# A delta-rule layer with a gated convolution: chunks of 32 tokens with the batches on four partition quadrants, in place of chunks of 64 with pairs of heads on two halves

## The chip, the core and the metric

The kernel runs on one core of a Trainium2 chip. The metric is the device time of one execution in microseconds (us). A core has five engines that run side by side, each through its own instructions in a fixed order: TensorE (PE, matrix products; its weight loads are listed as PEld), VectorE (DVE), ScalarE (ACT), GpSimd (POOL) and SyncE (SP, which here only issues DMA transfers). PE writes to PSUM, which this kernel uses in tiles of 128x512 (called banks in the code); ACT and DVE move results from there to SBUF. An fp32 product of the program appears in the trace as two matmul records, each with a weight load of its own; "record" below means one of these.

## The reference

Four batches, eight heads, 768 tokens, head size 48. A state matrix for each batch and head is read by the query and then corrected with the key and value of the token; what the queries read is the input of a gate, a causal convolution of five taps over tokens, applied to a projection.

```python
for t in range(S):
    kt, vt, bt = (k_n[:, :, t], v[:, :, t], beta[:, :, t, None])
    y[:, :, t] = np.einsum('bhd,bhde->bhe', q[:, :, t], state)
    v_old = np.einsum('bhde,bhd->bhe', state, kt)
    state = state + bt[:, :, :, None] * np.einsum('bhd,bhe->bhde', kt, vt - v_old)
...
for k in range(K):
    gate_pre += conv_w[k][None, None, :] * xp[:, k:k + S, :]
gate = 1.0 / (1.0 + np.exp(-gate_pre))
val = x @ w_val
return (gate * val @ w_out).astype(np.float32)
```

Here k_n is k divided by its length, and x is y with the eight heads side by side, 384 features a token.

## The kernel before

The loop over tokens is replaced by a loop over chunks. Inside a chunk the corrections of all tokens solve a triangular system, whose matrix comes from products of keys with keys (the gram). With the inverse of that matrix in hand a chunk needs four products: e, what the state says of the keys, taken off the values; u, the inverse applied to that; S, the state's update with keys and u; y, the queries on the state plus the masked products of queries and keys on u.

**Tiling.** A chunk is 64 tokens, and there are 12. Two heads share the 128 partitions, one on each half, so that 16 pairs (NP) stand along the free dimension. Two chunks make a group (128 tokens), and there are six groups.

**prep(g)** makes the inverses of a group. gram (L452, and gram0 for the first group) multiplies keys by keys and queries, and gevac copies the result to GL. diag picks the 32x32 diagonal blocks, trans_in turns them so that each partition of TLP holds one block per row of 1024 elements. Then the inverse TT_ is built on the free dimension: coef and cscale scale by beta over the squared length, row (L493) inverts blocks of 8, mergez8 and merget8 join them to 16, and zmul, zred, tmul and tred (L525 to L548) join 16 to 32, by a product with up to 1024 elements a partition and a sum over it. Some of the large products stand on POOL (buffers D1 and PR2), the others on DVE. trans_out turns the result twice, to TTR and TNA, and lev1 and lev2 join the 32-blocks to 64 on PE. bdcopy and tevac write the inverse to BD.

**chain(ch)** is the recurrence of one chunk: emul, eevac, umul, uevac, smul, sevac for the state, ymul and yevac for the output. Each product stands for one pair and one half; on PE two of them lie in different halves of the array. y comes out with features on partitions. yevac writes three quarters of it to X, and six DMA transfers a chunk (kind Lx) bring the rest to its partitions.

**moe(ch)** is the gate and the projection of a chunk: conv is tap 0 on ACT, tap is taps 1 to 3 on DVE (L783), tap_product on ACT and tap_sum on POOL (L790) are tap 4, sig the sigmoid, val (L798) nine products of 256 columns, gate (L802) the multiplication on DVE, outp (L809) six products of 384 columns, oevac the copy to SBUF, and then the output DMAs.

plan_weights turns the weights, which come as 64-bit numbers, into fp32: five steps on DVE and ACT, then f64_join, two multiplications and additions on POOL (L381, L382) for each of seven pieces.

**What sets the order.** Plan records every operation with its engine, an estimated cost and its tokens (what it reads and writes). Plan.order goes through the operations in time with these costs and puts on each engine, of those that are ready, the one with the highest rank (the longest way to the end plus a number of the table BIAS). The result is one fixed order for each engine. Where PE would stand idle, or has done little for some time, the planner adds keep_warm (L853), a product of zeros that changes nothing.

## Time and profile before

| what | value |
|---|---|
| median of 3 runs | 411.38 us (410.1 to 411.98) |
| span of the profiled execution | 416.2 us, 1.2% above that median |
| mean granted TensorE clock in it | 0.881 |
| PE, DVE, ACT, POOL busy | 352.4, 324.6, 233.7, 172.4 us |
| keep_warm among PE's time | 416 records, 62.6 us |
| moved by DMA | 45.31 MB, mean 109 GB/s; 44,576 of 59,805 packets under 512 bytes |

How to read it: PE's 352.4 us hold the fillers and whatever ran at a lowered clock, so they are not all work. A group's row in the profile gives the time in which at least one of its instructions ran, then the mean of one instruction; for products that lie in different parts of the array the first is far below the sum of the second.

### The profile page before, as it was taken

To read this page: it belongs to the slowest core of one execution; us is meant where nothing else is said; L and a number is where in the kernel's file an instruction comes from. 1 tells how busy PE (TensorE), PEld (TensorE's weight loads), DVE (VectorE), ACT (ScalarE), POOL (GpSimd) and SP (SyncE) were. 2 spreads that over 40 slices of the span, in tenths; PEclk is the share of its full clock that TensorE was granted. 3 is DMA by queue.
4 is the path that set the end of the run, shared out by engine and by line. 5 is a ranking of instruction groups with operands and counts; after the bars stand their busy time and mean duration, and the time that the engine had idled before them with its cause. 6 is when DMAs were issued, how large, how long until landed. Compare 5 with 4: busy or idle time off the path is not lost.

```text
span 416.2 us, 13720 instructions
## 1 busy us (share of the span) xinstructions
PE 352.4 (85%) x5836; PEld 297.6 (71%) x5836; DVE 324.6 (78%) x576; ACT 233.7 (56%) x509; POOL 172.4 (41%) x138
## 2 busy tenths in 40 slices
PE   8849967997499969989798999597599793999995
PEld 6849967886398738767586877476578593878883
DVE  5689999998894998988988379989587999320550
ACT  8403327966386636957377765353777364876420
POOL 4263650837802727505663233557023477100200
PEclk9985695999557969989989599989699997999999
DMA  7996561559273507354745545625303451010211
GB/s 222 166 251 198 157 183 50 145 151 192 52 151 116 142 14 157 104 122 139 154 106 157 128 130 142 106 61 131 49 2 79 78 114 24 2 41 13 48 39 38
DMA packets 59805, 45.31 MB, mean 109 GB/s; under 512 B 44576, under 2 KB 47776, under 8 KB 59744
## 3 DMA queue, kind: packets, MB, share of 16 engines
q1 hardware_dynamic: 59744, 44.43, 45.5%
q8 instruction: 46, 0.75, 0.8%
q14 instruction: 15, 0.12, 0.1%
HBM read 38.52 MB, written 4.72 MB: 104 GB/s over the span
## 4 chain that ended last, share of the span: by engine, by line
PE 52%; DVE 21%; DMA 11%; issue 6%; ACT 4%; SPq 3%; POOL 2%; DVEq 0%; POOLq 0%; ACTq 0%
PE gram L455 9%; PE SPS L853 9%; PE val L798 9%; PE out L809 8%; DVE GT L783 6%; PE u L713 4%; SPq L304 3%; DVE TTR L552 2%; DMA GL<-in_kq_dram 2%; PE SPS L725 2%; DMA AQ<-in_conv_w_dram 2%; PE z L564 2%; DVE TT__85 L547 2%; PE gram L465 2%; DVE PR L508 2%
## 5 line engine op out<-in xcount | busy, mean ns | idle before, releaser
L783 DVE SCALAR_TENSOR_TENSOR GT<-X,CW,GT 128x256 f32<-128x256 f32 x111 | 73.1, 684 | 12.9 <-POOL GT L790 12.2
L790 POOL TENSOR_TENSOR GT<-GT,TP 128x256 f32<-128x256 f32 x33 | 27.0, 817 | 97.7 <-ACT TP L299 97.4
L853 PE MATMUL SPS<-ZW 128*128 128x128 f32 x416 | 62.6, 309 | 0.0
L853 PEld LDWEIGHTS SPS<-ZW 128*128 128x128 f32 x416 | 58.5, 220 | 2.7 <-issue 1.0
L798 PE MATMUL val<-X,WV 128*128 128x256 f32 x216 | 58.9, 415 | 1.0 <-ACT BD L299 1.0
L809 PE MATMUL out<-WO,GT 128*128 128x384 f32 x144 | 52.1, 511 | 6.8 <-DVE GT L802 6.7
L455 PE MATMUL gram<-KQ,KBD 96*128 96x128 f32 x320 | 54.5, 331 | 0.8 <-DMA KQ<-in_kq_dram 0.8
L455 PEld LDWEIGHTS gram<-KQ,KBD 96*128 96x128 f32 x320 | 49.0, 237 | 2.3 <-ACT BD L299 0.9
L798 PEld LDWEIGHTS val<-X,WV 128*128 128x128 f32 x216 | 41.2, 203 | 7.6 <-ACT BD L299 1.1
L802 DVE TENSOR_TENSOR GT<-val,GT 128x256 f32<-128x256 f32 x36 | 15.0, 420 | 39.4 <-PE val L798 32.7
L575 ACT ACTIVATE BD<-TTR 32x512 f32<-32x512 f32 x48 | 30.1, 628 | 27.2 <-DVE TTR L552 26.7
L809 PEld LDWEIGHTS out<-WO,GT 128*128 128x128 f32 x144 | 27.4, 198 | 24.6 <-DVE GT L802 7.7
L449 POOL TENSOR_TENSOR US<-VT,NRM 64x768 f32<-64x768 f32 x24 | 36.4, 1516 | 19.7 <-DMA VT<-in_vt_dram 10.7
L299 ACT ACTIVATE GL<-gram 128x512 f32<-128x512 f32 x48 | 27.9, 594 | 23.4 <-PE gram L455 15.9
L793 ACT ACTIVATE GT<-GT 128x256 f32<-128x256 f32 x36 | 14.7, 415 | 43.4 <-DVE GT L783 43.1
L564 PE MATMUL z<-TTR,GL 32*32 32x32 f32 x768 | 12.0, 210 | 29.8 <-DVE TTR L552 21.6
L682 POOL TENSOR_SCALAR_AFFINE_SELECT AQ<-GL 64x1024 f32<-64x1024 f32 x24 | 28.7, 1195 | 15.4 <-PE y L739 8.9
L564 PEld LDWEIGHTS z<-TTR,GL 32*32 32x32 f32 x768 | 9.6, 123 | 34.0 <-DVE TTR L552 15.5
L713 PEld LDWEIGHTS u<-VT,BD 128*64 128x64 f32 x704 | 26.4, 157 | 9.5 <-ACT BD L299 4.5
L713 PE MATMUL u<-VT,BD 128*64 128x48 f32 x704 | 29.0, 242 | 4.5 <-ACT BD L299 3.6
L739 PE MATMUL y<-AQ,US 112*64 112x64 f32 x384 | 28.2, 226 | 1.8 <-ACT X L299 1.8
L299 ACT ACTIVATE OS<-out 128x384 f32<-128x384 f32 x24 | 11.8, 490 | 30.4 <-PE out L809 26.7
(116 smaller groups left out, 794.3 us busy)
## 6 DMA issues: line engine op xcount, KB each, us to landing
KBD<-in_kbd_dram SPq DMA_DIRECT2D x40, 192.0 KB, 3.1
KQ<-in_kq_dram SPq DMA_DIRECT2D x40, 192.0 KB, 3.3
KT<-in_kt_dram SPq DMA_DIRECT2D x12, 384.0 KB, 4.7
AQ<-in_qf_dram SPq DMA_DIRECT2D x24, 192.0 KB, 4.4
VT<-in_vt_dram SPq DMA_DIRECT2D x12, 384.0 KB, 3.7
out_dram<-OS SPq DMA_DIRECT2D x48, 96.0 KB, 2.2
KF<-in_kf_dram SPq DMA_DIRECT2D x22, 192.0 KB, 4.7
GL<-in_kq_dram SPq DMA_DIRECT2D x4, 448.0 KB, 9.6
```

Of the source, the lines that this page charges most:

```text
L299: A.activation(out=out, in_=in_, func=AF.Copy, **kw)
L449: G.tensor_tensor(out=USV[(2 * g + c) % 3][r, a], in0=VT[c][r].rearrange("p (h n) d -> p h n d", h=2), in1=n.unsqueeze(3).to_broadcast([64 ...
L455: PE.matmul(p[:, 128 * j:128 * (j + 1)], KBD[h % 2][:, j, :], KQ[h % 2][:, j, :], start=True, stop=True)
L564: PE.matmul(p[to:to + 32, x:x + 32], GL[r + 32:r + 64, u, 0:32], TTR[r + 32:r + 64, u, :], start=True, stop=True, tile_position=(r + 32, to))
L575: A.activation(out=BD[c][q:q + 32, :, q:q + 32], in_=TTR[q:q + 32, u0:u0 + NP, :], func=AF.Copy)
L682: G.affine_select(out=AQ[c][r0:r0 + 64, :, j, :], in_=GL[r0:r0 + 64, c * NP:(c + 1) * NP, 64:128], pattern=[[0, NP], [1, C]], compare_op=A ...
L713: PE.matmul(p[64 * a:64 * a + 64, D * j:D * j + D], BD[c][:, h * HB + j, 64 * a:64 * a + 64], VT[c][:, h * HB + j, :] if ch else us[:, a, ...
L739: PE.matmul(p[0:64, C * j:C * j + C], US[ch % 3][0:112, 0, h, D * j:D * j + 64], AQ[c][0:112, pp, 0, :], start=True, stop=True)
L783: eng.scalar_tensor_tensor(out=GT[m], in0=x[:, m, :, k:k + C], scalar=CW[:, m, k:k + 1], in1=GT[m], op0=ALU.mult, op1=ALU.add)
L798: PE.matmul(p[:, 0:B * C].rearrange("p (b t) -> p b t", t=C), WV[:, k, 128 * m:128 * m + 128], xs[:, k], start=(k == 0), stop=(k == NKT - 1))
L809: PE.matmul(bank["o", ch, i][:, 0:DM], GT[k][:, 2 * i:2 * i + 2, :].rearrange("p b t -> p (b t)"), WO[:, k, :], start=(k == 0), stop=(k == ...
L853: PE.matmul(SPS[0][:, 384:512], ZW, ZW, start=False, stop=True, skip_group_check=True)
```

## The change

The kernel is written anew around a step of 32 tokens. There are 24 steps, four to a group, and still six groups. Each of the four batches has its own quadrant of 32 partitions (quadrant b holds the 32 tokens of batch b), and the eight heads stand along the free dimension.

- **Chain.** estep, ustep, sstep, qstep and ystep are 32 products each (8 heads by 4 batches), and each product is addressed to one part of the array by tile_position: 64 rows by 32 columns in estep, qstep and gram, 32 by 32 in ustep and ystep, 32 by 64 in sstep. The four products of a head are issued one after the other. The values are subtracted on DVE (esum) where emul had an identity in its weights, and the state is moved by two sevac.
- **Inverse.** DVE goes to blocks of 16 only. pack and trans_out turn two blocks of 16, split writes them to RH and TZ, p1 and p2 (L517, L529) join 16 to 32 on PE with 128 products each a group, wsum on DVE stands between them. zmul, zred, tmul, tred, diag, lev1, lev2 and the second trans_out are gone.
- **Queries.** The mask on the products of keys and queries (ga) and vscale move from POOL to DVE.
- **Output.** y has tokens on partitions; flip turns it with three transposes on PE, and xevac copies it to X. The Lx transfers are gone.
- **Gate.** All four taps after the first stand on DVE (144 in place of 111); tap_product and tap_sum are gone. POOL keeps f64_join and halo.
- **Loads.** One tensor of keys and queries in rows of 8 KB replaces kq, kbd, kf and qf; the loads are for up to five chunks (NKQ = 5).
- **PSUM.** Six banks are named by the plan (PB) where two pools of three stood.
- **Plan.** New costs, a new table, one rule for fillers. The program holds 155 fillers; it held 208.

```diff
-        def zmul(eng, buf, kb):
-            n = 16 - 4 * kb
-            eng.tensor_tensor(
-                out=buf[:, 0:64 * n].rearrange("p (k i j) -> p k i j", k=4, i=16), op=ALU.mult,
...
-        def trans_out(w):
-            if w == 0:
-                V.transpose(out=TTR.rearrange("p u j -> p j u"), in_=tf.rearrange("p k j -> p j k"))
-            else:
-                V.transpose(out=TNA.rearrange("p u k -> p k u"), in_=tf)
...
-            for r in (0, 64):
-                add("ACT", 1.04, bdcopy, (c, r), r=["TTR"], w=[("BDd", c, r)])
...
-            if m in TAPS and not last:
-                add("ACT", 0.4, tap_product, (m,), r=XT_ + ["CW"], w=["TP"])
-                add("POOL", 0.7, tap_sum, (m,), r=["TP"], w=[gt])
...
+    def gram(s):
+        p, x, st = bank("g", s), KQ[s // 2 % NKQ], s % 2
+        for h in range(H):
+            for b in (0, 2, 1, 3):
+                r, a = 64 * (b // 2), b % 2
+                PE.matmul(p[32 * b:32 * b + 32, 64 * h:64 * h + 64], x[r:r + D, st, a, h, 0:T], x[r:r + D, st, a, h, :],
+                          start=True, stop=True, tile_position=(r, 32 * b))
...
+        def pack(b):
+            if b == 0:
+                copy(XL[:, :, 0:16], tf[:, 0:16, 0:16])
+            else:
+                copy(XL[:, :, 16:32], tf[:, 16:32, 16:32].rearrange("p k j -> p j k"))
+
+        def trans_out():
+            V.transpose(out=TX, in_=XL)
...
+        def p1(i):
+            p = bank("w", g)
+            for u in range(16 * i, 16 * i + 16):
+                for q in (0, 64, 32, 96):
+                    PE.matmul(p[q:q + 32, 16 * u:16 * u + 16], GD[gb][q:q + 32, u, :], RH[q:q + 32, u, :],
+                              start=True, stop=True, tile_position=(q, q))
...
+        def esum():
+            V.tensor_tensor(out=es, in0=vw(bank("e", s)), in1=vn[:, st], op=ALU.subtract)
+
+        def ustep():
+            p = bank("u", s)
+            for h in range(H):
+                for q in (0, 64, 32, 96):
+                    PE.matmul(p[q:q + 32, D * h:D * h + D], bd[q:q + 32, u0 + h, :],
+                              (es if s else vn[:, st])[q:q + 32, h, :], start=True, stop=True, tile_position=(q, q))
...
+        def sstep():
+            for h in range(H):
+                for b in (0, 2, 1, 3):
+                    r, a = 64 * (b // 2), b % 2
+                    PE.matmul(SPS[a][r:r + D, D * h:D * h + D], kt_[32 * b:32 * b + 32, st, h, :],
+                              us[32 * b:32 * b + 32, h, :], start=False, stop=True, skip_group_check=True,
+                              tile_position=(32 * b, r))
...
+        def flip():
+            p = bank("x", s)
+            for i in range(NKT):
+                PE.transpose(p[:, 128 * i:128 * i + 128], YS[s % 2][:, 128 * i:128 * i + 128], EYE)
```

In the rows below, a row is one or more equal instructions of one engine in the program's order: line, operation, what is written and read, size, count. The count is in products of the program, half the records of the trace.

PE ahead of the first u, before the change: lev1 is z, lev2 is t, and SPS<-ZW is the filler.

```order
L853 MATMUL SPS_120<-ZW 128x128 x6
L564 MATMUL z<-TTR,GL_81 32x32 x32
L853 MATMUL SPS_120<-ZW 128x128 x2
L455 MATMUL gram<-KQ_67,KBD_69 128x128 x4
L455 MATMUL gram<-KQ_68,KBD_70 128x128 x4
L853 MATMUL SPS_120<-ZW 128x128 x9
L585 MATMUL t_685<-ZS,TNA 32x32 x32
L455 MATMUL gram<-KQ_67,KBD_69 128x128 x4
L455 MATMUL gram<-KQ_68,KBD_70 128x128 x4
L564 MATMUL z<-TTR,GL_81 32x32 x16
L713 MATMUL u<-US_94,BD_92 64x48 x32
```

The same place now; RH,GD is p1, WS,TZ is p2, and the last row is ustep of step 0.

```order
L731 MATMUL SPS_138<-ZW 128x128 x27
L398 MATMUL PB_142<-KQ_65 32x64 x32
L731 MATMUL SPS_138<-ZW 128x128 x39
L517 MATMUL PB_143<-RH,GD_76 32x16 x128
L731 MATMUL SPS_138<-ZW 128x128 x5
L529 MATMUL PB_144<-WS,TZ 32x32 x64
L731 MATMUL SPS_138<-ZW 128x128 x2
L529 MATMUL PB_145<-WS,TZ 32x32 x64
L731 MATMUL SPS_138<-ZW 128x128 x2
L600 MATMUL PB_140<-VN_71,BD_96 32x48 x32
```

Six grams of the second group stood among the joining products of the first; now one gram of the third group is left here, those of the second stand earlier, and 75 of the 155 fillers stand in these ten rows.

PE in the middle of the program, before the change, around a u (the eight e, y or S products of a half are rows of their own and are cut off here).

```order
L853 MATMUL SPS_120<-ZW 128x128
L585 MATMUL t_1330<-ZS,TNA 32x32 x16
L853 MATMUL SPS_120<-ZW 128x128 x2
L455 MATMUL gram<-KQ_67,KBD_69 128x128 x4
L564 MATMUL z<-TTR,GL_82 32x32 x16
L455 MATMUL gram<-KQ_68,KBD_70 128x128 x4
L713 MATMUL u<-VT_75,BD_92 64x48 x16
L798 MATMUL val<-X_99,WV 128x256 x3
L713 MATMUL u<-VT_75,BD_92 64x48 x16
```

The middle of the program now, from one ystep (US,AQ) to the next ustep (ES,BD); ST,KQ is qstep at L622 and estep at L590, EYE,YS is flip, X,WV is val.

```order
L629 MATMUL PB_144<-US_101,AQ_79 32x48 x32
L681 MATMUL PB_141<-X_107,WV_116 128x256 x3
L398 MATMUL PB_142<-KQ_65 32x64 x32
L622 MATMUL PB_143<-ST_104,KQ_61 32x48 x32
L638 MATMUL PB_145<-EYE_132,YS_105 128x128 x3
L590 MATMUL PB_140<-ST_104,KQ_61 32x48 x32
L529 MATMUL PB_144<-WS_95,TZ_94 32x32 x64
L681 MATMUL PB_141<-X_107,WV_116 128x256 x3
L600 MATMUL PB_142<-ES_99,BD_96 32x48 x32
```

Between two stages of the chain that need each other there is now other work: val, a gram or p2 follows ystep and estep, where u was cut by one val.

DVE at the end of a group's inverse, before the change (ZT and TT_ are the products that join 16 to 32, GT the gate).

```order
L540 TENSOR_TENSOR PR<-ZT,TT__85 128x256
L547 TENSOR_REDUCE TT__85<-PR 128x16x4
L540 TENSOR_TENSOR PR<-ZT,TT__85 128x512
L547 TENSOR_REDUCE TT__85<-PR 128x16x4
L547 TENSOR_REDUCE TT__85<-PR_87 128x16x4
L802 TENSOR_TENSOR GT_104<-val,GT_104 128x256
L547 TENSOR_REDUCE TT__85<-D_83 128x16x4
L783 SCALAR_TENSOR_TENSOR GT_103<-X_101,CW,GT_103 128x256
L552 STREAM_TRANSPOSE TTR<-TT__85 128x32x32
L554 STREAM_TRANSPOSE TNA<-TT__85 128x32x32
```

The end of a group's inverse on DVE now (ES<-PB,VN is esum; the FA and FS rows belong to the weights).

```order
L481 TENSOR_TENSOR PR<-TLP,TT__88 128x256 x2
L485 TENSOR_REDUCE ZT<-PR 128x2x32
L368 SCALAR_TENSOR_TENSOR FA_129<-RAW_127,FA_129 128x384
L481 TENSOR_TENSOR PR<-TLP,TT__88 128x128 x2
L485 TENSOR_REDUCE ZT<-PR 128x2x32
L371 TENSOR_SCALAR FS_131<-FA_129 128x384
L491 TENSOR_TENSOR PR<-ZT,TT__88 128x128 x2
L496 TENSOR_REDUCE TT__88<-PR 128x2x8x4
L594 TENSOR_TENSOR ES_98<-PB_141,VN_72 128x384
L491 TENSOR_TENSOR PR<-ZT,TT__88 128x256 x2
L496 TENSOR_REDUCE TT__88<-PR 128x2x8x4
L505 STREAM_TRANSPOSE TX<-XL 128x512
```

The merge from 8 to 16 is now followed by the one short transposition; the rows that joined 16 to 32 have no counterpart on DVE.

## The prediction

> **What bounds the kernel now.** I read the page first, then the windows, the waits, and the timeline around one inverse.

> The page's busy line, DVE's row of the 40 slices, and the group of fillers:

> ```profile
> PE 352.4 (85%) x5836; PEld 297.6 (71%) x5836; DVE 324.6 (78%) x576; ACT 233.7 (56%) x509; POOL 172.4 (41%) x138
> ...
> DVE  5689999998894998988988379989587999320550
> ...
> L853 PE MATMUL SPS<-ZW 128*128 128x128 f32 x416 | 62.6, 309 | 0.0
> ```

> PE looks like the bound, but its 352 us hold 62.6 us of fillers and cold time. DVE stands at eight and nine tenths from slice 3 to 33.

> The windows of the steady part (four groups of 55 us; columns: length, PE, PEld, DVE, ACT, POOL, clock, DMA):

> ```profile
> 130.00:185.00 55.00, 48.71 (x891) 38.31 (x892) 51.44 (x88) 32.57 (x76) 27.14 (x20) 0.91 0.46 113
> 185.00:240.00 55.00, 49.53 (x862) 40.69 (x858) 42.96 (x65) 37.10 (x84) 26.34 (x19) 0.88 0.55 131
> 240.00:295.00 55.00, 43.72 (x730) 35.29 (x728) 50.43 (x86) 26.62 (x64) 27.23 (x21) 0.96 0.51 117
> 295.00:350.00 55.00, 44.75 (x892) 37.40 (x892) 46.14 (x83) 31.84 (x73) 25.40 (x19) 0.93 0.26 56
> sum 220.00, PE 186.71 PEld 151.70 DVE 190.97 ACT 128.13 POOL 106.12; mean PE 46.68 PEld 37.92 DVE 47.74 ACT 32.03 POOL 26.53
> ```

> DVE runs 191 of 220 us, 87%, and what PE waits for is DVE's inverse; from the view of waits:

> ```profile
> PE z L564 <- DVE TTR L552: 21.6, 3, 8.2
> PEld z L564 <- DVE TTR L552: 15.5, 2, 8.3
> ```

> So DVE sets the pace of a group, with PE close behind.

> **The first u.** The start is a stage of its own. DVE's timeline of the first group (transposition, end of the merge to 16, transposition of the finished 32-blocks), and the first u from the view of line 713:

> ```profile
> 22.66 2.11 DVE L478 STREAM_TRANSPOSE TLP<-D 128x1024 f32<-128x1024 f32 x1
> ...
> 42.04 0.69 DVE L523 TENSOR_REDUCE TT__85<-PR 128x64 f32<-128x512 f32 x1
> ...
> 63.09 1.92 DVE L552 STREAM_TRANSPOSE TTR<-TT__85 128x1024 f32<-128x1024 f32 x1
> ...
> L713 PE MATMUL u<-US,BD x64: 221/222/257, 76.5 to 78.6; 128*64 128x48 f32 x64
> ```

> Two pieces shrink. Between the end of the merge (42.7) and the first u (76.5) lie 33.8 us: the products that join 16 to 32 on DVE and POOL, two transpositions, z and t. Now there stand pack (two copies, 1.0), a half-size transposition (1.0), split (0.6), p1 (2.2), wsum (0.8), half of p2 (1.1), bd (0.6) and seven hand-overs of about 0.2: 8.7 us, priced from the rows further down.
> The part from L478 to that merge took 20.1 us. It gains the 17 coef steps (3.5), five ga (2.1) and the second group's transposition (2.1), and loses about 8: the weights' steps and the ops slowed by POOL in this stretch. So 20 again.
> The first transposition can begin when four grams are copied. Loads at the page's rate:

> ```profile
> GB/s 222 166 251 198 157 183 50 145 151 192 52 151 116 142 14 157 104 122 139 154 106 157 128 130 142 106 61 131 49 2 79 78 114 24 2 41 13 48 39 38
> ```

> 1.67 MB (beta and two chunks) at 222 GB/s are 7.5 us, then grams and copies: 14.5 in place of 22.7. Sum: 14.5 + 20 + 8.7 = 43. The values that the first u needs are behind 8.0 MB in SP's order (a piece of w_val among them, which ACT handles ahead of split): at 209 GB/s, the mean of four slices, 38 us plus the start. I take **45**; 42 if loads are quick, 52 if they come at 166 GB/s.

> **DVE afterwards.** What goes, by the view of lines:

> ```profile
> L540 DVE TENSOR_TENSOR PR<-ZT,TT__85 128x256 f32<-128x256 f32 (+2 forms) x13 | 23.0, 1766 | 0.3
> L527 DVE TENSOR_TENSOR PR<-TLP,TT__85 128x512 f32<-128x512 f32 (+2 forms) x13 | 15.2, 1166 | 0.2
> L534 DVE TENSOR_REDUCE ZT<-PR 128x64 f32<-128x768 f32 (+2 forms) x18 | 11.9, 682 | 0.3
> L547 DVE TENSOR_REDUCE TT__85<-PR 128x64 f32<-128x256 f32 (+2 forms) x18 | 11.8, 679 | 0.3
> L474 DVE SCALAR_TENSOR_TENSOR D<-GL,M,D 128x512 f32<-128x512 f32 x12 | 11.6, 967 | 0.4
> L554 DVE STREAM_TRANSPOSE TNA<-TT__85 128x1024 f32<-128x1024 f32 x6 | 11.5, 1922 | 0.0
> L473 DVE TENSOR_SCALAR D<-GL,M 128x512 f32<-128x512 f32 x12 | 8.5, 709 | 11.2 <-ACT GL L299 11.2
> L534 DVE TENSOR_REDUCE ZT<-D 128x64 f32<-128x1024 f32 x6 | 7.3, 1212 | 1.0 <-POOL D L527 1.0
> L547 DVE TENSOR_REDUCE TT__85<-D 128x64 f32<-128x1024 f32 x6 | 7.3, 1211 | 2.0 <-POOL D L540 2.0
> ```

> 108 us, and half of the remaining transposition, 6. What comes and what gets quicker:

> ```profile
> L783 DVE SCALAR_TENSOR_TENSOR GT<-X,CW,GT 128x256 f32<-128x256 f32 x111 | 73.1, 684 | 12.9 <-POOL GT L790 12.2
> ...
> L783 DVE SCALAR_TENSOR_TENSOR GT<-X,CW,GT x111: 389/484/2601, 115.2 to 401.4; 128x256 f32<-128x256 f32 x111
> ...
> L802 DVE TENSOR_TENSOR GT<-val,GT 128x256 f32<-128x256 f32 x36 | 15.0, 420 | 39.4 <-PE val L798 32.7 <-ACT BD L299 5.6 <-ACT ZS L299 1.1
> ```

> 33 taps at 0.48 are 16 us; 47 esum and vscale of 384 columns at about 0.6 (one and a half of L802's 0.42) 28; 24 ga at 0.42 10; wsum 4.5: 58. The tap's median is 0.48 but its mean 0.68 and its worst 2.6; long ones lie under POOL's products. With those gone, 111 taps get back about 22 us and the other short ops some 15. 324.6 - 114 + 58 - 37 = **232 us, 38 a group** against 54.

> **PE afterwards.** It becomes the bound. Rates at full clock, from timeline and chain of waits:

> ```profile
> 73.44 0.75 PE L585 MATMUL t<-ZS,TNA 32*32 32x32 f32 x64
> 74.12 0.38 PE L455 MATMUL gram<-KQ,KBD 96*128 96x128 f32 x1
> ...
> 212.50 0.20 PE L725 MATMUL SPS<-US,KT 64*48 64x48 f32 x1
> ...
> 212.95 0.21 PE L725 MATMUL SPS<-US,KT 64*48 64x48 f32 x1
> ...
> 213.09 1.56 PE L798 MATMUL val<-X,WV 128*128 128x256 f32 x6
> ...
> 402.96 3.88 PE val L798 x18
> 406.84 1.12 PE SPS L853 x10
> 407.96 3.88 PE out L809 x12
> ```

> The S products come in pairs in two array halves: ten pairs from 212.50 to 212.95, 45 ns a pair for 48 columns. t runs on four places at once: 64 records, less the change of shape, in 0.56 us, 8.7 ns each. So a set of four records of 48 columns on four places should take what a pair takes, 46 ns, and a stage of 64 records 16 x 46 = **0.74 us**. Below that the rate of t gives 0.56; above it 1.47, if sets of four ran as two pairs. I take 0.74, since t shows four at once. sstep is the least sure, as its tiles share columns two by two: up to 0.73 more in each of 23, 17 us. A gram of 64 columns is a third longer, 0.96; p1 and p2 are 512 records a group at 8.5, 4.35 us. Each change of shape costs about 0.1 (the step from S to val is 0.14, not 0.045). [...]

> After the first u, in the program's order: 117 stages 86; 15 grams 14; five groups of p1 and p2 22; flips 8; 12 chunks of val and of outp at 3.88 each 93; 202 changes of shape 20. **244 us**, without fillers. The same list before is no longer: PE's work does not shrink, the wait for DVE does.

> PE will not run at full clock without gaps. In the windows above it was busy 85% (fillers included) at a clock of 0.92, with DVE as the bound. I take the same 0.92, and 0.92 busy, as esum and the three copies of a step stand behind val, gram or qstep in PE's order. One stage of a step then needs 0.74 + 0.2, its copy 0.48 by this row:

> ```profile
> L718 ACT ACTIVATE US<-u 64x384 f32<-64x384 f32 x24 | 11.6, 483 | 15.7 <-PE u L713 15.2
> ```

> Three stages, esum, three copies and hand-overs are about 6 us a step, 144 in all, so the recurrence is not the limit. The weak place is early: by the third group's short transposition DVE has 91 us of work in its order and started near 13, PE reaches that group's p1 at 45 + 65 = 110. Until about 100 us POOL still runs fourteen products of the weights:

> ```profile
> L381 POOL TENSOR_TENSOR WV<-WV,GT 128x384 f32<-128x384 f32 x2 | 2.4, 1180 | 4.9 <-ACT GL L299 2.6 <-DVE QUOT L425 2.3
> ```

> At 1.2 us each they can slow DVE by up to 10 us there; this is why I don't take more than 0.92. Behind the last outp come a copy and this transfer, 3 us:

> ```profile
> out_dram<-OS SPq DMA_DIRECT2D x48, 96.0 KB, 2.2
> ```

> Sum: 45 + 244 / 0.92 / 0.92 + 3 = 45 + 288 + 3 = 336 us of span. The span before, 416.2, stands 1.2% above the median of the runs, so 336 x 0.988 = **332**; I say 333.

> [...]

> **The rivals.**
> 1. The fixed orders don't meet: engines wait for each other as before, 85% busy, clock 0.88 (the worst of the four windows). 45 + 244 / 0.85 / 0.88 + 3 = 374, or 370. For it: PE, DVE and ACT each alternate between two jobs. Against: DVE keeps 30% of its time free.
> 2. PE is nearly full: 0.96 and 0.96, 43 + 265 + 3 = 311, or 307. For it: other work lies between any two dependent stages. Against: the early part.
> 3. Slower: four tiles of a set don't run side by side, in pairs only. Stages, grams, p1 and p2 double: 122 us more, 45 + 366 / 0.846 + 3 = 481, or 475. It decides against the change from 67 us on, where these sets take 1.55 times as long. Against it: t.
> 4. Slower: the clock stays down. The small tiles give PE less to do, and the windows show what follows an idle PE:

> ```profile
> 102.90:109.70 6.80, 0.00 (x0) 0.00 (x0) 5.51 (x5) 0.00 (x0) 6.74 (x6) 0.50 0.42 83
> 109.70:130.20 20.50, 19.94 (x252) 17.41 (x252) 14.38 (x39) 16.05 (x31) 4.94 (x6) 0.50 0.49 108
> ```

> PE was busy 19.9 of 20.5 us with little in the array, and the clock did not rise. At a mean of 0.72 the gain is gone (244 / 0.92 / 0.72 = 368); at 0.6 the span is 490. Against it: val and outp, 93 us, are spread over all steps.

> **How the numbers follow.** Forecast (315 to 357) 0.55; rival 1 (357 to 395) 0.24; rival 2 (295 to 315) 0.13; rival 3 0.05; rival 4 0.03. The range from 305 to 385 leaves out rivals 3 and 4 and the ends of 1 and 2, near 0.17. Half a per cent is about what a measurement of this kernel can tell from no change: faster by more 0.91, within it 0.01, slower 0.08.

> **What would show it.** The first ustep near 45. DVE near 232 us in all, taps near 0.48. A stage's 64 records in 0.74 us. PE over 90% busy after the first u, its largest waits on DVE before 110 us. The forecast is wrong if sets of four come at 92 ns, if the clock after the start is under 0.85, or if p1 waits for DVE in every group.

## The result, and the profile after

The changed kernel is slower: **466.4 us** median of 6 runs (464.1 to 470.2), against 411.1 (408.4 to 414.9) for the kernel before on the same chip. The ratio is 1.136, with a 95% interval from 1.129 to 1.143. The forecast was 333 us, with a range up to 385 us. The profiled execution of after has a span of 468.1 us. Executions of one kernel fall into a faster and a slower group, and every ratio below is taken from the faster ones alone, so a ratio and a median need not agree.

From the page of after: the busy line, DVE's row and PE's granted clock in 40 slices, the queue that brings instructions (q8: packets, MB, share), the chain of what ended last, and the groups of taps and fillers.

```profile
PE 369.2 (79%) x12842; PEld 296.7 (63%) x12842; DVE 206.9 (44%) x581; ACT 137.0 (29%) x292; POOL 16.9 (4%) x31
...
DVE  3137663543756455266013383210387772041351
...
PEclk9677977777887979788579778877899979989899
...
q8 instruction: 100, 1.64, 1.4%
...
PE 76%; issue 19%; DMA 2%; DVE 1%; SPq 0%; ACT 0%
...
L672 DVE SCALAR_TENSOR_TENSOR GT<-X,CW,GT 128x256 f32<-128x256 f32 x144 | 60.9, 479 | 51.2 <-ACT GT L308 50.7
...
L731 PE MATMUL SPS<-ZW 128*128 128x128 f32 x310 | 56.5, 334 | 5.2 <-issue 5.2
```

And the same queue on the page of before:

```profile
q8 instruction: 46, 0.75, 0.8%
```

DVE is relieved as forecast (206.9 us busy, forecast 232; taps 0.479 us) and is no longer the bound. But PE is busy only 79% of the span, and 19% of the chain is "issue": PE waited for nothing that the profile names. In the view of waits, the largest of PE's:

```profile
PE PB L517 <- issue: 16.5, 7, 4.9
PE PB L600 <- issue: 15.9, 7, 6.5
PE PB L398 <- issue: 13.3, 5, 6.0
PE PB L529 <- issue: 13.0, 9, 2.3
PE PB L622 <- issue: 11.1, 7, 2.0
```

Where these waits lie is seen in PE's timeline (start, length, what ran, records, and in brackets the idle time ahead of it):

```profile
125.09 1.07 PE L529 MATMUL PB<-WS,TZ 32*32 32x32 f32 x103 [2.26 <-issue]
126.09 1.56 PE L681 MATMUL PB<-X,WV 128*128 128x256 f32 x6
127.59 0.44 PE L600 MATMUL PB<-ES,BD 32*32 32x48 f32 x19
128.55 0.70 PE L600 MATMUL PB<-ES,BD 32*32 32x48 f32 x45 [0.52 <-issue]
129.18 0.94 PE L731 MATMUL SPS<-ZW 128*128 128x128 f32 x6
130.04 0.93 PE L610 MATMUL SPS<-US,KT 32*48 32x48 f32 x64
130.91 0.36 PE L629 MATMUL PB<-US,AQ 32*32 32x48 f32 x13
132.00 0.78 PE L629 MATMUL PB<-US,AQ 32*32 32x48 f32 x51 [0.73 <-issue]
132.71 1.10 PE L398 MATMUL PB<-KQ 48*32 48x64 f32 x64
133.74 0.49 PE L731 MATMUL SPS<-ZW 128*128 128x128 f32 x2
134.16 0.35 PE L590 MATMUL PB<-ST,KQ 48*32 48x48 f32 x11
136.00 0.79 PE L590 MATMUL PB<-ST,KQ 48*32 48x48 f32 x53 [1.49 <-issue]
```

PE stops in the middle of a stage whose other products ran a moment ago. From one stop to the next: 103 + 6 + 19 = 128 records; 45 + 6 + 64 + 13 = 128; 51 + 64 + 2 + 11 = 128. From its first product on PE stands idle for over 0.4 us 46 times, 90.8 us together. Two of these gaps, ahead of 13 us, wait for keys and queries (2.7 us); the other 44, with 88.1 us, follow each other at 128 records or a multiple, at 13 of the 43 distances one less (26 semaphore instructions of PE lie in that stretch, two for each of the 13), and each ends 1.2 to 1.8 us after a packet of the queue q8 has ended.

Queue q8 explains the number. Its 100 packets carry 1.64 MB, 16 KB each. PE has 12842 matmul records and as many weight loads, 25684 instructions: some 256 to a packet, 1.64 MB / 25684 = 64 bytes each, so 128 records with their weight loads fill one **piece** of 16 KB. In the trace a packet of q8 begins about 1.1 us after PE entered the piece ahead (median 1.11 of 100, 96 of them after that moment), takes 1.05, and the first record that it holds starts 1.4 us after its end. So in this trace a piece is fetched once the one before it is entered, and the next stop ends some 3.45 us after the last (125.09, 128.55 and 132.00 above). The eleven such distances in the trace with no load in the way lie between 3.3 and 4.3 us, six of them over 3.7; 3.45 is near the lower end. 128 small records run in 1.4 us; then PE waits. Dense products hide this: records of val start 216 ns apart at full clock in after, so 128 of them would run some 28 us, an estimate.

**My theory**: the instruction supply sets the pace, 100 pieces in place of 46. **Rivals**: (A) the stops come from the program's own waits; (B) tiles or PSUM accesses collide; (C) PE's own work at its clock sets the time; (D) the low clock is the cause, and the stops follow from it; (E) the written order is at fault; and for the versions with few pieces, (F) PE's own work is again the limit.

### The profile page after: what moved, and what is told of

Read it like the earlier page. It is cut to its first block, busy times and chain, and to the rows that moved or that the text cites. A ratio compares the mean times of both kernels' runs of the same rounds, so it can differ in the third digit from the quotient of the medians.

```text
span 468.1 us, 26967 instructions
## 1 busy us (share of the span) xinstructions
PE 369.2 (79%) x12842; PEld 296.7 (63%) x12842; DVE 206.9 (44%) x581; ACT 137.0 (29%) x292; POOL 16.9 (4%) x31
## 3 DMA queue, kind: packets, MB, share of 16 engines
q8 instruction: 100, 1.64, 1.4%
## 4 chain that ended last, share of the span: by engine, by line
PE 76%; issue 19%; DMA 2%; DVE 1%; SPq 0%; ACT 0%
PE PB L681 13%; PE PB L689 12%; PE SPS L731 11%; PE PB L398 6%; PE PB L600 6%; PE SPS L610 5%; PE PB L629 5%; PE PB L590 4%; PE PB L622 4%; PE PB L529 4%; PE PB L517 4%; PE PB L638 3%; DMA KQ<-in_kq_dram 2%; SPq L311 0%; DVE VN L538 0%
## 5 line engine op out<-in xcount | busy, mean ns | idle before, releaser
L681 PE MATMUL PB<-X,WV 128*128 128x256 f32 x216 | 64.6, 451 | 0.9 <-DVE PR L473 0.7
L731 PE MATMUL SPS<-ZW 128*128 128x128 f32 x310 | 56.5, 334 | 5.2 <-issue 5.2
L689 PE MATMUL PB<-WO,GT 128*128 128x384 f32 x144 | 59.3, 556 | 0.0
L731 PEld LDWEIGHTS SPS<-ZW 128*128 128x128 f32 x310 | 47.9, 233 | 9.2 <-issue 7.0
L681 PEld LDWEIGHTS PB<-X,WV 128*128 128x128 f32 x216 | 46.1, 224 | 9.7 <-issue 1.2
L398 PE MATMUL PB<-KQ 48*32 48x64 f32 x1536 | 31.6, 237 | 16.0 <-issue 13.3
L398 PEld LDWEIGHTS PB<-KQ 48*32 48x32 f32 x1536 | 27.0, 120 | 21.7 <-issue 17.8
L689 PEld LDWEIGHTS PB<-WO,GT 128*128 128x128 f32 x144 | 28.8, 212 | 17.5 <-issue 5.3
L600 PE MATMUL PB<-ES,BD 32*32 32x48 f32 x1472 | 26.9, 228 | 15.9 <-issue 15.9
L600 PEld LDWEIGHTS PB<-ES,BD 32*32 32x32 f32 x1472 | 22.6, 124 | 22.4 <-issue 20.6
L622 PE MATMUL PB<-ST,KQ 48*32 48x48 f32 x1472 | 23.7, 213 | 11.1 <-issue 11.1
L610 PEld LDWEIGHTS SPS<-US,KT 32*48 32x48 f32 x1472 | 22.5, 135 | 15.5 <-issue 13.4
L517 PE MATMUL PB<-RH,GD 32*32 32x16 f32 x1536 | 18.9, 189 | 16.5 <-issue 16.5
L610 PE MATMUL SPS<-US,KT 32*48 32x48 f32 x1472 | 26.1, 223 | 6.5 <-issue 6.4
L308 ACT ACTIVATE US<-PB 128x384 f32<-128x384 f32 x24 | 11.8, 491 | 62.1 <-PE PB L600 62.0
L517 PEld LDWEIGHTS PB<-RH,GD 32*32 32x32 f32 x1536 | 17.2, 118 | 19.4 <-issue 18.5
L529 PE MATMUL PB<-WS,TZ 32*32 32x32 f32 x1536 | 18.6, 202 | 13.0 <-issue 13.0
L622 PEld LDWEIGHTS PB<-ST,KQ 48*32 48x32 f32 x1472 | 20.2, 114 | 13.6 <-issue 12.6
```

The lines of the kernel that those rows point to most:

```text
L308: A.activation(out=out, in_=in_, func=AF.Copy, **kw)
L398: PE.matmul(p[32 * b:32 * b + 32, 64 * h:64 * h + 64], x[r:r + D, st, a, h, 0:T], x[r:r + D, st, a, h, :], start=True, stop=True, tile_pos ...
L517: PE.matmul(p[q:q + 32, 16 * u:16 * u + 16], GD[gb][q:q + 32, u, :], RH[q:q + 32, u, :], start=True, stop=True, tile_position=(q, q))
L529: PE.matmul(p[q:q + 32, 32 * j:32 * j + 32], TZ[q:q + 32, u, :], WS[q:q + 32, u, :], start=True, stop=True, tile_position=(q, q))
L600: PE.matmul(p[q:q + 32, D * h:D * h + D], bd[q:q + 32, u0 + h, :], (es if s else vn[:, st])[q:q + 32, h, :], start=True, stop=True, tile_p ...
L610: PE.matmul(SPS[a][r:r + D, D * h:D * h + D], kt_[32 * b:32 * b + 32, st, h, :], us[32 * b:32 * b + 32, h, :], start=False, stop=True, ski ...
```

## The experiments

Differences from after are taken from the ratios to before: (ratio - 1.136) x 411 us. The intervals make them uncertain by about 4 to 7 us. Where no ratio stands, only the median and the range are known. Twelve kernels ran.

**The stop by itself.** Behind the whole program:

```
quads(SPS[0], 512, 48)      # 32x32 products on four places, 48 columns
whole(SPS[1], 256, 48)      # 128x128 products
quads(SPS[0], 512, 8)
whole(SPS[1], 128, 256)
...
for c in range(4):
    for r in range(2):
        load(KQ[c][64 * r:64 * r + D], kq[c, r])
quads(SPS[0], 512, 48)
```

> Behind the whole program of after, with no data in flight, PE gets five bursts: 512 products of 32x32 on four places with 48 columns (1024 records), 256 whole products of 128x128 with 48 columns (512 records), 512 on four places with 8 columns (1024 records), 128 whole products with 256 columns, and the first burst again with eight loads of about 393 KB issued ahead of it. Theory (PE's instructions come in pieces of 16 KB, 128 records of products and their weight loads, and each piece takes 3.45 us from the request to the first product that it holds, one piece ahead only): first burst 8 pieces x 3.45 = 27.6 us, stalls at every 128th record; the burst with 8 columns also 27.6 us although it streams a sixth; whole products of 48 columns at about 40 ns a record, 20 us, and those of 256 at 216 ns, 55 us, both without stalls; the last burst 30 us or more, its first stalls 2 to 5 us longer than in the first burst. Rival A (the stalls belong to the program's waits and to its order on other engines): first and last burst 1024 x 10.8 ns = 11.1 us, no stalls. Rival B (tiles or PSUM accesses collide now and then): the stalls don't come at every 128th record, and fewer columns make them smaller.

Timeline of PE in that stretch:

```profile
475.82 1.56 PE L743 MATMUL SPS<-US,BD 32*32 32x48 f32 x128 [2.46 <-issue]
479.56 1.56 PE L743 MATMUL SPS<-US,BD 32*32 32x48 f32 x128 [2.18 <-issue]
483.58 1.21 PE L743 MATMUL SPS<-US,BD 32*32 32x48 f32 x88 [2.46 <-issue]
484.72 109.46 PE L748 MATMUL SPS<-YS,EYE 128*128 128x48 f32 x512
594.12 2.42 PE L743 MATMUL SPS<-US,BD 32*32 32x8 f32 x168
597.57 1.89 PE L743 MATMUL SPS<-US,BD 32*32 32x8 f32 x128 [1.03 <-issue]
...
621.34 57.05 PE L748 MATMUL SPS<-YS,EYE 128*128 128x256 f32 x256
...
684.56 1.65 PE L743 MATMUL SPS<-US,BD 32*32 32x48 f32 x128 [3.78 <-issue]
695.71 2.79 PE L743 MATMUL SPS<-US,BD 32*32 32x48 f32 x128 [9.50 <-issue]
```

The first burst took 28.0 us (456.73 to 484.72) and the one with 8 columns 27.2, against 27.6 forecast for both, with a stop at every 128th record; nothing here waits for another engine, and a sixth of the columns saves nothing. That excludes A and B as the cause. The totals agree better than the price: from stop to stop it is 3.5 to 4.0 us, and the first 168 records of each burst ran without a stop, as a piece had come during the dense products ahead of them. Behind the loads a stop grew to 9.5 us. The whole products ran without a stop, but those of 48 columns took 214 ns a record and not 40: a miss of mine, taken up in the last section.

**Columns or records.** The gram's products, twice as wide or twice as many:

```
-  PE.matmul(p[.., 64 * h:64 * h + 64], x[r:r + D, st, a, h, 0:T], x[r:r + D, st, a, h, :], ...)
+  PE.matmul(p[.., 64 * h:64 * n], x[r:r + D, st, a, h, 0:T], x[r:r + D, st, a, h:n, :], ...)   # n = min(h + 2, H)
```

> The 28 of 32 products of a gram that aren't of the last head stream 128 columns in place of 64; the next head's product overwrites what is too much. As many instructions as after, 448 more columns on each of four places in 24 grams: 56 records x 14 ns = 0.78 us each, 19 us in all at full clock. Theory (instruction supply): hidden in the stalls, as 128 records of a wide gram take 3.6 us, about what a piece of the program takes to come; the time within 8 us of after's, perhaps less by a higher clock. Rival C (PE's own work and clock set the time): 19 to 23 us more than after.

```
+  for _ in range(2 if h < H - 1 else 1):
       PE.matmul(p[.., 64 * h:64 * h + 64], ...)
```

> The same 28 products of each gram are issued twice with 64 columns: as many columns more as in the wide gram, and 24 x 56 = 1344 records more, 10.5 pieces of 128. Theory (instruction supply): 10.5 x 3.5 to 4.3 us = 37 to 45 us more than after. Rival C (PE's own work and clock): 19 to 23 us more, as much as the wide gram.

Wide: 471.6 us, ratio 1.139 (1.124 to 1.155), 1 us more than after. Twice: 510.9 us, 1.232 (1.225 to 1.238), 39 us more. Both stream the same columns; only the second adds instructions, and its page counts the pieces:

```profile
q8 instruction: 111, 1.82, 1.5%
```

11 pieces for 39 us: 3.6 us each. This is what separates the theory from C.

**Loads and pieces.**

```
-  add("SP", dma(393), load, (KQ[k][64 * r:64 * r + D], kq[c, r]), ...)
+  add("SP", dma(393), load if c < NKQ else skip, (KQ[k][64 * r:64 * r + D], kq[c, r]), ...)   # VN and KT alike
```

> The loads of keys, queries and values of chunks 5 to 11 are left out (the order of the rest is unchanged; those chunks compute with what the buffers hold). Theory (instruction supply, and pieces that are requested while a load is in flight are late): the five stalls of 3 to 6.5 us between 109 and 303 us and the one near 91 lose 2 to 4 us each: 15 to 22 us less than after. Rival A or C: no change by over 3 us, since no instruction of after waits long for those loads.

447.2 us, ratio 1.088 (1.082 to 1.095), 20 us less. In after, the DMA view of 109.4 to 115.6 us (GB/s in 40 slices) shows what stands ahead of the one packet of q8 there:

```profile
GB/s 159 211 211 211 211 211 53 159 145 93 99 79 119 119 119 231 139 198 238 317 297 278 159 145 59 20 0 0 0 0 0 0 0 0 0 0 0 0 0 0
DMA packets 193, 0.66 MB, mean 107 GB/s; under 512 B 33, under 2 KB 33, under 8 KB 161
...
q8 instruction: 1, 0.02, 1.1%
```

and the timelines the stop at its end, in after and without the loads:

```profile
115.57 1.41 PE L517 MATMUL PB<-RH,GD 32*32 32x16 f32 x90 [3.03 <-issue]
```

```profile
107.03 1.41 PE L520 MATMUL PB<-RH,GD 32*32 32x16 f32 x90 [1.64 <-issue]
```

PE entered the piece ahead at 109.4, but the packet began only at 113.1, as the loads ended.

**Fewer records, same products, same order.** Two batches in one product of 64x64 weights with two 32x32 blocks on the diagonal, first in ustep and ystep, then in p1 and p2:

```
-  for q in (0, 64, 32, 96):
-      PE.matmul(p[q:q + 32, ..], bd[q:q + 32, u0 + h, :], es[q:q + 32, h, :], ..., tile_position=(q, q))
+  for q in (0, 64):
+      PE.matmul(p[q:q + 64, ..], bd[q:q + 64, u0 + h], es[q:q + 64, h, :], ..., tile_position=(q, q))
```

> The same order on every engine, but ustep and ystep take two batches in one product: BD and AQ hold two 32x32 blocks on the diagonal of a 64x64 weight, the moving columns stay 48, so a stage is 32 records in place of 64. 1536 records less, 12 pieces of 128; ACT gets 12 copies of 0.6 us more, DVE's ga writes twice the columns (5 us in all). Theory (instruction supply): faster than after, at most by 12 x 3.45 = 41 us, less where these stages lie beside val and outp, whose 216 ns a record cover the fetch: 10 to 41 us less than after. Rival C (PE's own work, clock): the records stream as long as before, so no gain; 0 to 10 us more than after by the additional copies.

> The same order, ustep and ystep as in after, but p1 and p2 with two batches in one product of 64x64 weights (GP and TZ hold the blocks on the diagonal; ACT writes GP by two more copies of 0.38 us in each gk, and TZ by two copies). Also 1536 records less, 12 pieces, but these stand in bursts of 256 to 512 with nothing dense between them. Theory (instruction supply): 12 x 3.45 = 41 us less than after if every one of the twelve was a stall, 25 to 45 us less in all, and more than the pairs of ustep and ystep bring. Rival C (PE's own work, clock): no gain, or up to 18 us more by ACT's copies.

ustep and ystep: 451.5 us (447.2 to 475.5), ratio 1.081 (1.070 to 1.092), 22 us less. p1 and p2: 423.8 us, 1.023 (1.015 to 1.031), 46 us less, nearly four microseconds for each of twelve pieces. From the page with pairs in p1 and p2, and its window from the first ustep to the last outp (length, PE, PEld, DVE, ACT, POOL, clock, DMA):

```profile
PE 366.8 (87%) x11306; PEld 302.0 (72%) x11306; DVE 207.4 (49%) x590; ACT 160.5 (38%) x347; POOL 16.9 (4%) x31
...
q8 instruction: 88, 1.44, 1.4%
...
PE 84%; issue 11%; DMA 3%; DVE 1%; SPq 0%; ACT 0%
...
71.80:418.00 346.20, 309.53 (x10275) 249.83 (x10274) 173.41 (x467) 140.47 (x304) 13.28 (x21) 0.92 0.23 52
```

and its timeline at the p2 that had stopped up to 125.09 in after:

```profile
120.23 3.92 PE L543 MATMUL PB<-WS,TZ 64*64 64x32 f32 x128
124.08 1.56 PE L695 MATMUL PB<-X,WV 128*128 128x256 f32 x6
```

The pairs stream slower, not faster: 128 of them take 3.9 us, which covers the fetch of the next piece, and the stop is gone. In that window PE is idle for 36.7 us (346.20 - 309.53), where after has 77.2 (its window is in the next section): 40 of the 46 us are idle time that went. The same number of records taken out of two places brings 22 and 46 us, which agrees with pieces costing most where nothing dense stands between.

**The clock.**

```
 def keep_warm():
-    PE.matmul(SPS[0][:, 384:512], ZW, ZW, start=False, stop=True, skip_group_check=True)
+    pass
```

> After without its 155 fillers (310 records, 2.4 pieces; they add zero to columns that nothing reads). Theory (instruction supply sets the pace, the clock's drop follows from the stalls and is mostly covered by them): 0 to 14 us less than after, although the granted clock falls below 0.84. Rival D (the clock is the cause, and stalls only follow from it): slower than after by over 10 us, since the fillers are what keeps the array at work in the stalls.

459.9 us, ratio 1.109 (1.100 to 1.119), 11 us less than after: against D. Its view of cores, and its window from the first ustep to the last outp, read

```profile
core 0: 458.0 us, clock 0.854
...
66.20:455.00 388.80, 302.88 (x11462) 238.72 (x11451) 173.93 (x469) 125.97 (x271) 13.63 (x21) 0.83 0.20 47
```

against 0.840 for all of after and 0.84 in its window. The 0.854 doesn't mean that the clock held: this trace has no clock reading before 74.8 us, and 128 records of gram took 3.63 us there, 28 ns each, where after's grams start 26.1 ns apart at clock 0.50 and 14.1 at full clock. So by estimate PE ran these at about half clock, and from the first ustep on at 0.83, hardly lower than after. Its other runs show 0.763, 0.776 and 0.872, and all four took 456.8 to 460.1 us.

**The order.** In four kernels the planner was told of the pieces and its table searched again; a fifth keeps after's order. Their core:

```
+  def pe(self, t, cost, cols, n=2):            # n: records
+      ...
+      if not self.left:
+          t, self.left = max(t, self.come), PIECE
+          self.come = t + COME + min(max(0.0, self.pipe - t - 1.1), LATE)
```

and for all four pairs in after's order, besides `pass` in keep_warm, GP behind pack:

```
+  for j in range(2):
+      copy(GP[0][:, :, j, :], GD[gb], scale=PM[:, j:j + 1])     # PM: 1 on the quadrants of half j
```

> After's own products and tiles, 31 fillers in place of 155, and a new order: the planner is told that every 128 records of PE must wait for a piece that is requested when the last one was entered and comes 3.5 us later (up to 4 us later still behind a load), and its bias table is searched again under that rule. 98 pieces in place of 100. Theory (instruction supply): the order can put dense products between bursts, but the number of pieces stays: 98 x 3.45 = 338 us and what the start and the loads add, so 410 to 440 us, faster than after (466) and not faster than before (411). Rival E (the order written in after is the fault, and the supply only a part of it): under 400 us.

> The pairs of p1 and p2 (a product of 64x64 weights for two batches; GP is written from GD by two ACT copies) and an order searched under the same rule: about 87 pieces. Theory (instruction supply): 87 x 3.45 = 300 us is no longer the limit everywhere; 390 to 410 us, 15 to 30 us less than the reordered kernel without pairs. Rival C (PE's own work): not faster than that kernel, since p1 and p2 stream 3 us a group longer.

> Pairs in p1, p2, ustep and ystep, 7 AQ buffers in place of 9 to make room, one GP buffer, and an order searched under the same rule: about 76 pieces, 76 x 3.45 = 262 us. Theory (instruction supply): PE's own work (about 290 us) is now longer than the pieces take, so 365 to 395 us, faster than before's 411. Rival C (PE's own work and clock set the time): 420 us or more, since no record's work was taken away and the pairs stream 29 ns a record where quads take 10.8.

> The same products as the reordered kernel with pairs in p1, p2, ustep and ystep; only the order differs: the bias table is searched for the mean of three settings (a piece comes after 3.4, 3.55 or 3.8 us, other engines 0, 5 or 10% slower), so that an engine that runs late meets other work. About 76 pieces. Theory (instruction supply, now below PE's own work, so that the order of the start and the waits count): 380 to 405 us, 2 to 8% faster than before. Rival F (what is left is PE's own work at the clock that it gets, whatever the order): 405 to 415 us, as the kernel ordered for one setting.

> Three of the edits together in after's own order: pairs in ustep and ystep, pairs in p1 and p2 (GP is one buffer here, written from GD by two ACT copies of 1 us behind pack), and no fillers. Against after (466) these brought 15, 43 and 6 us one at a time. Theory (instruction supply): 73 pieces; if the gains add up 466 - 64 = 402 us, and 395 to 412 us in all, so faster than before or as fast. Rival F (PE's own work at the clock that it gets is now the limit): 410 to 425 us, since pairs stream longer and without fillers nothing holds the clock.

| kernel | us, median (range) | ratio to before (95%) |
|---|---|---|
| after's products, new order | 450.2 (440.9 to 453.1) | |
| pairs in p1, p2, new order | 436.0 (428.4 to 446.0) | 1.046 (1.036 to 1.055) |
| all four pairs, new order | 411.7 (405.7 to 417.5) | 0.992 (0.986 to 0.998) |
| all four pairs, order for three settings | 416.8 (410.0 to 422.4) | |
| all four pairs, after's order, no fillers | 420.7 (414.4 to 425.8) | 1.011 (1.000 to 1.022) |

All five missed the time that the theory had forecast. The first came out 10 us above its range, and far from E's 400: it is 16 us under after, where leaving out the fillers had alone given 11, so the written order is at most a small part. The second is 14 us under the first, where C had it no faster, but slower than after's order with the same pairs (423.8): that searched order is not better. Which wait makes that one slower was not tried. The last three end together, at 412 to 421 us with 74 or 75 pieces, whatever the order. From the page of the fastest, and the windows of the fastest and of the last one from the first ustep to the last outp:

```profile
PE 368.1 (90%) x9646; PEld 305.8 (75%) x9646; DVE 213.7 (52%) x592; ACT 171.7 (42%) x359; POOL 16.2 (4%) x31
...
q8 instruction: 75, 1.23, 1.3%
...
PE 79%; DMA 7%; DVE 6%; issue 5%; ACT 1%; SPq 1%; DVEq 0%
```

```profile
64.90:406.00 341.10, 318.91 (x8810) 261.06 (x8808) 177.59 (x484) 149.48 (x315) 4.48 (x13) 0.89 0.21 49
```

```profile
70.90:413.00 342.10, 316.50 (x8629) 262.28 (x8626) 178.91 (x468) 148.73 (x297) 13.94 (x21) 0.86 0.23 52
```

In both, PE is busy 93% of the time after the first u (316.5 of 342.1 us in the last one, at a clock of 0.86 and without fillers), and "issue" is 5% of the fastest one's chain, against 19% in after. This agrees with F: with 74 pieces the supply is no longer what takes most, PE's work is, and the gains of single edits don't add up (22 + 46 + 11 = 79 us singly, 51 together). The pairs have their price there: 316.5 x 0.86 = 272 us of work at full clock, against 245 in after (worked out in the next section). The forecast of 365 to 395 us for the fastest took 290 us for PE's work; PE was busy 318.9 us and idle 22.2 more after the first u. F's two ranges, 405 to 415 and 410 to 425 us, were missed by 2 us and met. The best version is 0.8% faster than before, a little over the half per cent that can be told from no change. No version beat before clearly.

## Why the prediction was wrong

**The step that failed** is the quotient in "Sum: 45 + 244 / 0.92 / 0.92 + 3": PE was to be 0.92 busy because its records would follow each other at the rates read from t and S. The supply of instructions was in none of the terms and in none of the four rivals. What the quotient became is in the windows of after from the first ustep to the last outp: all of PE, and L731 alone.

```profile
69.70:465.00 395.30, 318.15 (x11555) 250.85 (x11554) 173.32 (x467) 125.59 (x271) 13.24 (x21) 0.84 0.20 46
...
69.70:465.00 395.30, 26.95 (x115) 20.04 (x114) 0.84 0.20 46
```

395.3 us in place of 288. Without fillers PE was busy 318.15 - 26.95 = 291.2 us at 0.84, which is 245 us at full clock: **the 244 us were right**. That is not a sum of errors that cancel: from the starts of the records, each weighted with the clock of its moment, stages take 98 us (forecast 86 and some 12 of changes), grams 15 (14), p1 and p2 25 (22), val and outp 100 (93) and flips 10 (8). No run shows the 8 us that the sum has for 24 flips; a flip is three records in after, 0.33 to 0.48 us a step at full clock. The 107 us too many are three parts. Idle time: 77.2 us in place of 23, +54; the stops at pieces in this stretch are 39 with 73.7 us. The clock: 291.2 - 265 = +26. Fillers: +27, which stand mostly in time that PE would have waited anyway, since leaving them out gave 11 us. The lower clock goes with the stops: 0.84 here, and with twelve pieces fewer in p1 and p2 that kernel's window above shows 0.92, as forecast.

**The first u** came at 69.7, not 45. It is the same cause at one remove. While 1.4 MB of loads were in flight, a gram stopped for 5.99 us at 13.9, and later ones for 1.80 and 2.87 us. In DVE's order, products of the second group's grams (L407) stand ahead of the first group's inverse, so DVE waited with them:

```profile
22.31 1.94 DVE L432 STREAM_TRANSPOSE TLP<-GD 128x1024 f32<-128x1024 f32 x1 [7.49 <-ACT GD L308]
...
28.01 0.42 DVE L407 TENSOR_TENSOR AQ<-PB,MASK 128x256 f32<-128x256 f32 x1 [3.36 <-ACT GD L308]
...
36.24 0.42 DVE L407 TENSOR_TENSOR AQ<-PB,MASK 128x256 f32<-128x256 f32 x1 [5.33 <-ACT GD L308]
```

The first transposition is 7.8 us later than the forecast's 14.5, and 8.7 us follow in these two waits. Between p1 at 55.6 and ustep stand 14 us in place of about 6, with three more stops and a low clock. The "20 again" of DVE's own steps is not contradicted. This part is read from the trace and not tried: no run changed the loads of the start, and in all the versions the first u stands between 58.7 and 71.8 us.

**Right**: DVE no longer the bound (207 us, 25 under the 232 of the forecast), flips near their term, tail 3 us. Rival 3 is false: sets of four come at 10.8 ns a record, sstep at 11.6; a stage that doesn't stop takes 0.82 us to the next product (69.69 to 70.51 for the first ustep), where 0.74 and 0.1 for the change of shape were forecast. Rival 4's sign was right and its mechanism was not: 0.84 is under the 0.85 that I had named as the mark, but the clock is 26 of the 132 us and rose to 0.92 when pieces were taken out. Rival 1 had PE waiting for other engines; it waited for its own instructions. p1 writes from four places into one bank at 8.9 ns a record, and within a piece sets of 48 columns come at 10.8. Yet a small record costs some 27 ns or more where nothing dense stands between (27.2 us for 1024 of 8 columns behind the program), as the pieces set the pace there.

**It could have been seen.** Before's page has the 46 packets with 0.75 MB; the number of records more than doubles with the new tiles. What a packet costs stood in no row of before, where few runs of small products are longer than 128 records; the t records, from which the rate was read, are 64. Its view of lines has 9.0 us of "issue" ahead of z's weight loads, which looks like a sign of it and is not one, as most of it is this wait in PEld's timeline:

```profile
65.13 0.97 PEld L564 LDWEIGHTS z<-TTR,GL 32*32 32x32 f32 x64 [6.63 <-issue]
```

It ends just as DVE's transposition into TTR is done (63.09 + 1.92 = 65.01), and the last packet of q8 was then 9 us old.

## What to carry to other kernels

Count PE's instructions before counting its columns: 128 small records, with their weight loads, cost 3.3 us or more here however little they streamed (28.0 us for 1024 of 48 columns, 27.2 for 1024 of 8), so where nothing dense stands between them a finer tiling bought nothing below some 27 ns a record. Two blocks on the diagonal of one wider weight, which stream longer and halve the instructions, gained 46 us in the place where small products stood alone. Keep long loads out of such stretches: behind them the next piece of program began 3.2 to 5.0 us after the one ahead was entered, in place of 1.1, and without them the kernel took 20 us less.
